# Rows 0 to 5 of a retention and MLP kernel in another form, and the last conversions of w_out placed behind the last burst

## The chip, the cores and the metric

The kernel runs on one core of a Trainium2 chip. The metric is the device time of one execution in microseconds, as a median over runs; a profile of one execution gives the span from its first to its last instruction, engine by engine. The engines are TensorE (PE; its weight loads are listed as PEld), VectorE (DVE), ScalarE (ACT), GpSimd (POOL) and SyncE (SP), which here issues most of the loads.

## The reference

Two computations follow each other. The first is an attention with a decaying state, for 4 batches, 8 heads, 768 tokens and head dimension 64, in float32:

```python
for t in range(S):
    state = gamma * state + einsum("bhd,bhe->bhde", k[:, :, t], v[:, :, t])
    y[:, :, t] = scale * einsum("bhd,bhde->bhe", q[:, :, t], state)
```

`gamma` is 1 - 2**(-5 - head), `scale` is 1/8. The second takes y as x, 3072 tokens of 512 values (8 heads by 64), and computes

```python
h = x @ w_in                      # 512 x 2048
g = h * clip(h + 3, 0, 6) / 6
out = g @ w_out                   # 2048 x 512
```

## The kernel before

**Rows.** The 3072 tokens are 24 rows of 128 tokens, six to a batch. For each row the kernel makes the scores `sc` (keys by queries), multiplies them by a mask that holds decay or causality (`weigh`, result `am`), and sums two parts into `y`: the inner part, from `am` and the values `vn`, and the past part, from the queries and the state. The keys and values of the row are added into the state's PSUM tile `uz` (`sums`), and ACT copies it to a `state` tile in SBUF (`keep`, line 388). A row is worked in two chunks of 64 tokens, so that it needs two state copies, and every product is of 64x64. All these products are issued by `together` (line 384), which deals several lists of products out by turns. In rows 0 to 7 the values are scaled by a decay (`decay`, POOL at line 322 for the rows in ONPOOL, ACT at line 325 for the others) and y by another (`xr`, DVE, line 525); from row 8 on GpSimd scales the keys (line 312) and the queries (line 316, with the table `dq` that SP loads) ahead of the products. Then x is split into a high part (ACT, line 196) and a low part (DVE, line 199), both fp32r.

**h.** Four rows are a unit of 512 tokens; there are six. A weight block of w_in arrives as 64-bit floats in a staging tile `st` (two of them) and is converted by DVE and ACT (lines 160 to 183: `a` and `b` take exponent and mantissa with a mask, `e` is ACT's, then `q`, `f`, `w`) and split into high and low. A tile of h is one block of 128 columns of w_in by one unit: 12 products of 128x128 by 128x512 (line 431: four slices of the inner dimension, and three products of high and low for each). There are 96 tiles. ACT adds 3 and takes the relu (line 438), DVE takes the minimum with 6 and multiplies by h (`times`, line 442), and a DMA that ACT issues stores the tile in DRAM (`gd`, line 465). `finish` is these three steps for one tile.

**o.** The second matrix product (1008 products, line 698) goes over three blocks of 1024 tokens. Each is formed with seven products of half matrices in place of eight, in four groups: (4, 5), (1, 6), (7), (2, 3). A group takes four pieces c0 to c3 of g. A piece is loaded by two SP DMAs into a `gv` tile (lines 668, 671, 673), added or subtracted in DVE (lines 119, 116), and split into a `gc` tile (ACT line 196, DVE line 199). The gv tiles take three places in turn: one in the pool `late`, and `gv0` and `gv1`, which lie in the memory that the staging pool `wst` leaves when phase one ends. The weights of w_out are converted like those of w_in in 16 blocks, with four differences of quarter blocks more (`build_w2`, letters `1230`, and `g k h l` for the splits). Ten of them are made in the long stretch of h, the last six (10 to 15) in unit 5, at tiles 4, 6, 8, 10, 12 and 14 (WHEN).

**What sets the order.** The string HEAD is a fixed list for the first two units: each word is a step (a letter for the step, the row or block or unit.block behind it), and PE, DVE, ACT and SP take their instructions in that order. `steady` does the same for units 2 to 4, with a `chunk_burst` for a row after every fourth tile. In unit 5 and in the o part only PE keeps the written order; a scheduler places the instructions of the others, by priority and by what they depend on, and fixes each engine's list when the kernel is built. Each engine, SP's queue of loads included, takes its list strictly in order. `read` limits the loads in flight to 10 KB in each partition. The stores of h tiles stand in ACT's list behind the next relu (`issue_after`).

Of the kernel before, what the change touches and what calls it, by code (L numbers as in the profile page):

```python
# [30 lines left out]
def retention_ffn(ctx: ExitStack, tc: tile.TileContext, qkv, w_in, w_out, dkc, dqc, dmc, tab, out, B, H, S, D):  # L31
# [784 lines left out]
```

## Time and profile before

| | |
|---|---|
| median of 3 runs | 579.28 us (579.1 to 579.87) |
| profiled execution: own time, span | 581.04 us, 579.3 us |
| PE busy | 565.8 us (98%) |
| DVE busy | 423.8 us (73%) |
| ACT busy | 247.1 us (43%) |
| POOL busy | 45.4 us (8%) |
| on the chain that ended last | h products 44%, o products 40%, the rows' products y, sc, uz 9% together |
| mean DMA rate | 200 GB/s |

A row of the timeline gives start, duration, engine, line, operation, what it writes and reads with shapes, and in square brackets the idle time before it with what ended it. Rows of groups give a count (x1008), the busy time, the mean of one in ns, and the idle time ahead of them. Buffer numbers are left out of the names. A plain float32 product stands in the trace as two passes. The granted clock (PEclk) is TensorE's clock as a share of its full speed.

### The profile page before, as it was taken

To read this page: it belongs to the slowest core of one execution; us is meant where nothing else is said; L and a number is where in the kernel's file an instruction comes from. 1 tells how busy PE (TensorE), PEld (TensorE's weight loads), DVE (VectorE), ACT (ScalarE), POOL (GpSimd) and SP (SyncE) were. 2 spreads that over 40 slices of the span, in tenths; PEclk is the share of its full clock that TensorE was granted. 3 is DMA by queue.
4 is the path that set the end of the run, shared out by engine and by line. 5 is a ranking of instruction groups with operands and counts; after the bars stand their busy time and mean duration, and the time that the engine had idled before them with its cause. 6 is when DMAs were issued, how large, how long until landed. Compare 5 with 4: busy or idle time off the path is not lost.

```text
span 579.3 us, 12415 instructions
## 1 busy us (share of the span) xinstructions
PE 565.8 (98%) x5126; PEld 463.5 (80%) x5126; DVE 423.8 (73%) x588; ACT 247.1 (43%) x368; POOL 45.4 (8%) x51
## 2 busy tenths in 40 slices
PE   7799999999999999999999999999999999999997
PEld 5677887888888888888788888888888888888885
DVE  5489998733677678777726989679776698866871
ACT  3285544432444444434324555543434343344430
POOL 3201011121111111112000000000000000000000
PEclk9799999999999999999999999999999999999999
DMA  8866777835665666666542576465754757636611
GB/s 267 289 212 218 251 250 241 272 132 182 208 212 204 209 218 222 232 221 233 204 158 92 180 246 226 149 216 164 272 180 115 247 148 258 214 107 189 213 74 72
DMA packets 58324, 115.82 MB, mean 200 GB/s; under 512 B 5782, under 2 KB 6678, under 8 KB 58268
## 3 DMA queue, kind: packets, MB, share of 16 engines
q1 hardware_dynamic: 44144, 89.67, 48.1%
q10 hardware_dynamic: 14124, 25.37, 11.6%
q8 instruction: 40, 0.66, 0.5%
q14 instruction: 16, 0.13, 0.1%
HBM read 83.56 MB, written 31.46 MB: 199 GB/s over the span
## 4 chain that ended last, share of the span: by engine, by line
PE 92%; DMA 5%; issue 1%; DVE 1%; SPq 0%; POOL 0%; DVEq 0%
PE h L431 44%; PE o L698 40%; PE y L384 3%; PE sc L384 3%; PE uz L384 3%; DMA early<-in_qkv 2%; DMA st<-in_w_in 2%; DMA qt<-in_qkv 1%; SPq L136 0%; DVE we L160 0%; DVE wb L172 0%; DVE x L199 0%; POOL early L322 0%; DVE xr L525 0%; DVE we L177 0%
## 5 line engine op out<-in xcount | busy, mean ns | idle before, releaser
L431 PE MATMUL h<-x,w 128*128 128x512 f32 x1152 | 270.1, 393 | 0.4 <-ACT w L196 0.3
L431 PEld LDWEIGHTS h<-x,w 128*128 128x128 f32 x1152 | 214.0, 188 | 46.9 <-ACT w L196 0.7
L698 PE MATMUL o<-gc,w 128*128 128x512 f32 x1008 | 230.7, 391 | 0.0
L698 PEld LDWEIGHTS o<-gc,w 128*128 128x128 f32 x1008 | 189.2, 188 | 41.3
L438 ACT ACTIVATE g<-h,three 128x512 f32<-128x512 f32 x96 | 65.8, 687 | 104.2 <-PE h L431 97.6
L442 DVE SCALAR_TENSOR_TENSOR g<-g,h 128x512 f32<-128x512 f32 x96 | 65.5, 684 | 54.8 <-ACT g L438 54.7
L196 ACT ACTIVATE gc<-gv 128x1024 fp32r<-128x1024 f32 x48 | 50.9, 1060 | 63.1 <-PE o L698 56.4
L199 DVE TENSOR_TENSOR gc<-gv,gc 128x1024 fp32r<-128x1024 f32 x48 | 58.6, 1221 | 23.5 <-ACT gc L196 23.5
L196 ACT ACTIVATE gc<-spare 128x1024 fp32r<-128x1024 f32 x36 | 38.2, 1062 | 49.6 <-PE o L698 40.2
L199 DVE TENSOR_TENSOR gc<-spare,gc 128x1024 fp32r<-128x1024 f32 x36 | 43.9, 1221 | 10.3 <-ACT gc L196 10.3
L169 ACT ACTIVATE we<-we,ebias 128x512 int32<-128x512 int32 x32 | 23.0, 719 | 22.2 <-DVE we L160 22.2
L388 ACT ACTIVATE state<-uz 128x256 f32<-128x256 f32 x45 | 17.2, 382 | 29.8 <-PE y L384 16.0
L196 ACT ACTIVATE w<-ww 128x384 fp32r<-128x384 f32 (+2 forms) x34 | 18.6, 552 | 24.3 <-DVE ww L183 23.7
L183 DVE SCALAR_TENSOR_TENSOR ww<-wb,we 128x512 f32<-128x512 f32 x32 | 24.3, 760 | 0.9
L172 DVE SCALAR_TENSOR_TENSOR wb<-st,wb 128x512 f32<-128x512 uint32 x32 | 22.9, 717 | 0.8
L177 DVE SCALAR_TENSOR_TENSOR we<-st,we 128x512 int32<-128x512 int32 x32 | 23.1, 721 | 0.0
L316 POOL TENSOR_TENSOR qs<-qt,dq 128x512 f32<-128x512 f32 x16 | 22.3, 1394 | 3.3 <-DMA dq<-in_decays_q 3.3
L199 DVE TENSOR_TENSOR w<-ww,w 128x384 fp32r<-128x384 f32 (+2 forms) x34 | 20.0, 593 | 2.6 <-ACT w L196 2.5
L160 DVE TENSOR_SCALAR we<-st 128x512 int32<-128x512 int32 x32 | 13.5, 421 | 8.4 <-DMA st<-in_w_in 5.5
L116 DVE TENSOR_TENSOR spare<-spare,gv 128x1024 f32<-128x1024 f32 x12 | 14.7, 1222 | 5.7 <-DMA gv<-gd 5.7
L384 PE MATMUL y<-qs,state 64*64 64x64 f32 x480 | 18.3, 222 | 0.0
L384 PE MATMUL y<-am,vn 64*64 64x64 f32 x512 | 18.2, 219 | 0.0
(66 smaller groups left out, 427.6 us busy)
## 6 DMA issues: line engine op xcount, KB each, us to landing
gd<-g ACTq DMA_DIRECT2D x96, 256.0 KB, 3.0
gv<-gd SPq DMA_DIRECT2D x48, 512.0 KB, 4.8
gv<-gd SPq DMA_DIRECT2D x48, 256.0 KB, 3.1
st<-in_w_in SPq DMA_DIRECT2D x16, 512.0 KB, 4.4
st<-in_w_out SPq DMA_DIRECT2D x16, 512.0 KB, 4.8
early<-in_qkv SPq DMA_DIRECT2D x28, 256.0 KB, 4.3
kt<-in_qkv SPq DMA_DIRECT2D x16, 256.0 KB, 3.4
qt<-in_qkv SPq DMA_DIRECT2D x16, 256.0 KB, 4.1
```

The costliest lines, as they stand in the source:

```text
L169: nc.scalar.activation(out=t["e"], in_=t["e"], func=AF.Relu, scale=8.0, bias=ebias)
L172: nc.vector.scalar_tensor_tensor(out=t["b"].bitcast(F32), in0=lo.bitcast(U32), scalar=2.0**-32, in1=t["b"], op0=ALU.mult, op1=ALU.add)
L177: nc.vector.scalar_tensor_tensor(out=t["e"], in0=hi, scalar=-2147483648, in1=t["e"], op0=ALU.bitwise_and, op1=ALU.bitwise_or)
L183: nc.vector.scalar_tensor_tensor(out=t["w"], in0=t["b"].bitcast(F32), scalar=2.0**-20, in1=t["e"].bitcast(F32), op0=ALU.mult, op1=ALU.mult)
L196: nc.scalar.activation(out=hi, in_=src, func=AF.Copy)
L199: nc.vector.tensor_tensor(out=lo, in0=src, in1=hi, op=ALU.subtract)
L316: nc.gpsimd.tensor_tensor(out=t["qs"], in0=t["qt"], in1=d, op=ALU.mult)
L384: nc.tensor.matmul(out_, lhs, rhs, start=start, stop=True, skip_group_check=True)
L431: nc.tensor.matmul(h, t[:, o, a], xs[u][b][:, k], start=k + n == 0, stop=(k, n) == (NK - 1, 2), skip_group_check=True)
L438: return g, nc.scalar.activation(out=g, in_=h, func=AF.Relu, bias=three).ins
L442: ins = nc.vector.scalar_tensor_tensor(out=g, in0=g, scalar=6.0, in1=h, op0=ALU.min, op1=ALU.mult)
L698: nc.tensor.matmul(acc[i][h] if last else acc[i][:, h], w2c[j][:, RIGHT[i], x, h], gc[:, y, jj], start=j == 0 and n == 0, stop=j == NFP - ...
```

## The change

It has two parts. In the first, rows 0 to 5 are worked whole, 128 tokens at a time. The scores of a row are eight products of 64x128 and eight of 64x64, in an `sc` of two PSUM banks; the mask is 128 wide, and `weigh` multiplies 128x1024 at once. The inner part and the past part are eight products each, the sums eight, with one state copy for each row. The sums of the last row of a batch (row 5) are left out, and its kn isn't read. The values of these rows are laid out by token and scaled with a table `vcst` of their own. Rows 6 and 7, which were in the form of rows 0 to 5, take that of the later rows: GpSimd scales their keys and queries. ONPOOL goes from rows 0 to 4 to rows 1 to 3. One buffer of h tiles in PSUM goes to the scores (ps_h 4 to 3). HEAD is a new list, with other letters for the new steps: O scores, Y past, U inner, N sums, D load of dq, G and R the scaling of keys and queries.

In the second part `build_w2` is given the instruction behind which its first operation has to stand: the last `finish` ahead of it.

```diff
-    ONPOOL = (0, 1, 2, 3, 4)
+    OLD = TROWS
+    ONPOOL = (1, 2, 3)
     HEAD = """
-        L0 L1 F L2 L3 L4 F L5 L6 T0 T1 C0 T3 c0 T4 C1 C3 s0 d0 C4 T5 T2 p0 C5 A0 m0 C2 c1 z1 S1 d1 y0 m1 B0 x0 p1 a0
...
+        L0 L1 F L2 L3 F L4 T1 T0 C1 T2 T4 c0 C2 T3 T5 O0 C4 d0 C5 m0 C0 U0 c1 B0 C3 N0 d1 U1 x0 O1 B1 a0 X0 b0 Y2 q0
...
-    mask = const.tile([P, NPAIR, D], F32, name="mask")
+    mask = const.tile([P, 2, NPAIR // 2, P], F32, name="mask")
...
-    ps_h = ph1.enter_context(tc.tile_pool(name="ps_h", bufs=4, space=PSUM))
+    ps_h = ph1.enter_context(tc.tile_pool(name="ps_h", bufs=3, space=PSUM))
...
-    def build_w2(n):
+    def build_w2(n, after):
         steps = w2_steps(n, fetch(w_out[divmod(n, 2)]))
-        for k in "abeqfw1230gkhl":
+        with tc.issue_after(after):
+            steps["a"]()
+        for k in "beqfw1230gkhl":
             steps[k]()
...
-    sc = ps_a.tile([P, NPAIR, P], F32, name="sc")
+    sc = ps_a.tile([P, 2, NPAIR, P], F32, name="sc")
+    nc.vector.memset(sc, 0.0)
...
+            m = NPAIR * P
+            if x == "kn" and r % ROWS_B == ROWS_B - 1:
+                m = m // 2 if r >= OLD else 0
+            if not m:
+                continue
...
+    def load_q(r):
+
+        d = rows[r]["dqc"] = apool.tile([P, NPAIR, P], F32, tag="dq", name=nm("dq"), bufs=1)
+        read(d.rearrange("p h n -> p (h n)"), dqc[r % ROWS_B])
...
+    def whole_scores(r):
+
+        t, todo = rows[r], []
+        for p in range(NPAIR):
+            for c in range(2):
+                for h, pr in enumerate(halves):
+                    tokens = slice(0, P) if c == 0 else halves[1]
+                    to = sc[halves[h ^ p % 2 ^ c], h, place_am(p, h), tokens]
+                    todo.append((to, t["kt"][pr, p, halves[c]], t["qt"][pr, p, tokens], True))
+        together(todo)
+
+    def whole_past(r):
+
+        y, state, q = both["y"][:, r % 2], before[2 * r], rows[r]["qt"]
+        together([(y[halves[1 - h], p], state[pr, p], q[pr, p], p == 0) for p, h, pr in sides])
+
+    def whole_inner(r):
+
+        t, y = rows[r], both["y"][:, r % 2]
+        first = r % ROWS_B == 0
+        together([(y[halves[1 - h], p], t["vn"][:, p, pr], both["am"][:, h, place_am(p, h)], first and p == 0) for p, h, pr in sides])
+
+    def whole_sums(r):
+
+        t, first = rows[r], r % ROWS_B == 0
+        together([(uz[pr, p], t["kn"][:, p, pr], t["vn"][:, p, pr], first and p == 0) for p, h, pr in sides])
+
+    def whole_weigh(r):
+
+        nc.vector.tensor_tensor(
+            out=both["am"].rearrange("p h a n -> p h (a n)"),
+            in0=sc.rearrange("p h a n -> p h (a n)"),
+            in1=mask.rearrange("p a b n -> p (a b n)")[:, None, :].to_broadcast([P, 2, NPAIR * P]),
+            op=ALU.mult,
+        )
...
             for tile_ in pending[:-1]:
-                finish(*tile_)
+                last = finish(*tile_)
...
-        steady()
+        end = steady()
...
         if jj in WHEN:
-            build_w2(n_w2)
+            build_w2(n_w2, end)
             n_w2 += 1
         end = finish(*tile_of_h(u, jj))
```

The lists of three engines show where this moves instructions. The first is DVE's around the border between the last h tiles and the o part. L442 (now L498) is `times`; `we`, `wb`, `ww`, `ws` are the tiles of a conversion, here of block 15; `w2` is the converted block; `spare` and `gc` belong to pieces of g, whose c0 has gv_517 before and gv_511 now. Before:

```order
L116 TENSOR_TENSOR ws_510_4215<-ww_509_4213,ws_510_4215 128x128
L442 SCALAR_TENSOR_TENSOR g_503_4183<-g_503_4183,h_502_4170 128x512
L116 TENSOR_TENSOR ws_510_4215<-ws_510_4215,ww_509_4213 128x128
L199 TENSOR_TENSOR w2_497_4151<-ww_509_4213,w2_497_4151 128x3x128
L199 TENSOR_TENSOR w2_497_4151<-ws_510_4215,w2_497_4151 128x4x128
L119 TENSOR_TENSOR spare0_4293<-gv_517_4300 128x1024
L442 SCALAR_TENSOR_TENSOR g_505_4200<-g_505_4200,h_504_4187 128x512
L199 TENSOR_TENSOR gc_519_4307<-spare0_4293,gc_519_4307 128x1024
L442 SCALAR_TENSOR_TENSOR g_512_4237<-g_512_4237,h_511_4224 128x512
L442 SCALAR_TENSOR_TENSOR g_514_4254<-g_514_4254,h_513_4241 128x512
L119 TENSOR_TENSOR spare0_4293<-gv_520_4334 128x1024
L199 TENSOR_TENSOR gc_521_4338<-gv_520_4334,gc_521_4338 128x1024
```

Now, where g_506 and g_508 are the last two tiles of h, gv_520 is piece c3, gv_514 is c1, and the first row is block 15's first operation:

```order
L164 TENSOR_SCALAR we_501_4051<-st_500_4049 128x512
L168 TENSOR_SCALAR wb_502_4053<-st_500_4049 128x512
L498 SCALAR_TENSOR_TENSOR g_506_4082<-g_506_4082,h_505_4069 128x512
L176 SCALAR_TENSOR_TENSOR wb_502_4053<-st_500_4049,wb_502_4053 128x512
L181 SCALAR_TENSOR_TENSOR we_501_4051<-st_500_4049,we_501_4051 128x512
L498 SCALAR_TENSOR_TENSOR g_508_4099<-g_508_4099,h_507_4086 128x512
L187 SCALAR_TENSOR_TENSOR ww_503_4058<-wb_502_4053,we_501_4051 128x512
L123 TENSOR_TENSOR spare1_4139<-gv_520_4247 128x1024
L120 TENSOR_TENSOR ws_504_4060<-ww_503_4058 128x128 x2
L120 TENSOR_TENSOR ws_504_4060<-ww_503_4058,ws_504_4060 128x128
L203 TENSOR_TENSOR w2_491_3996<-ww_503_4058,w2_491_3996 128x3x128
L120 TENSOR_TENSOR ws_504_4060<-ws_504_4060,ww_503_4058 128x128
```

Block 15's operations, which stood ahead of the last three `times` with its splits done, now stand among and behind the last two, and behind them come the sum and the split of c3.

The second place is SP's list of loads at the same border. The st tiles are w_out's blocks, L668 (now L716) loads pieces of the first group, L673 (now L721) pieces of the second group. Before, where gv_520, gv_523 and gv_526 are c1, c2 and c3:

```order
L136 DMA st_496_4149<-in_w_out 128x512
L136 DMA st_506_4204<-in_w_out 128x512
L668 DMA gv_520_4334<-gd2_65 128x2x512
L668 DMA gv_520_4334<-gd3_66 128x2x512
L668 DMA gv_523_4368<-gd4_67 128x2x512
L668 DMA gv_523_4368<-gd5_68 128x2x512
L668 DMA gv_526_4402<-gd6_69 128x2x512
L668 DMA gv_526_4402<-gd7_70 128x2x512
L673 DMA gv_531_4440<-gd0_63 128x512
L673 DMA gv_531_4440<-gd1_64 128x512
```

Now, where gv_520 is c3, gv_514 is c1, gv_517 is c2, and gv_531 is c2 of the second group, in the place in `late` that c3 has held:

```order
L140 DMA st_490_3994<-in_w_out 128x512
L140 DMA st_500_4049<-in_w_out 128x512
L716 DMA gv_520_4247<-gd6_69 128x2x512
L716 DMA gv_520_4247<-gd7_70 128x2x512
L721 DMA gv_531_4353<-gd4_67 128x512
L716 DMA gv_514_4179<-gd2_65 128x2x512
L716 DMA gv_514_4179<-gd3_66 128x2x512
L716 DMA gv_517_4213<-gd4_67 128x2x512
L716 DMA gv_517_4213<-gd5_68 128x2x512
L721 DMA gv_531_4353<-gd5_68 128x512
L721 DMA gv_525_4285<-gd0_63 128x512
```

The loads of c1 and c2 moved behind those of c3 and behind the first load of the second group's c2.

The third place is GpSimd's list in the first part of the program. `early` are tiles of rows 0 to 7, am_1 serves as a kn tile. Before:

```order
L322 TENSOR_TENSOR early_3_120<-early_3_120,ccst_71 128x256 x4
L322 TENSOR_TENSOR early_6_132<-early_6_132,ccst_71 128x256 x4
L322 TENSOR_TENSOR early_8_142<-early_8_142,ccst_71 128x256 x2
L312 TENSOR_TENSOR kn_68_878<-kn_68_878,ccst_71 128x512
L316 TENSOR_TENSOR qs_70_883<-qt_66_874,dq_69_881 128x512
L312 TENSOR_TENSOR am_1_118<-am_1_118,ccst_71 128x512
L316 TENSOR_TENSOR qs_99_1043<-qt_96_1035,dq_98_1041 128x512
```

Now:

```order
L348 TENSOR_TENSOR early_3_125<-early_3_125,vcst_71 128x256 x2
L348 TENSOR_TENSOR early_6_137<-early_6_137,vcst_71 128x256 x4
L328 TENSOR_TENSOR early_23_278<-early_23_278,ccst_73 128x512
L334 TENSOR_TENSOR qs_44_550<-early_23_278,dq_24_284 128x512
L328 TENSOR_TENSOR kn_36_459<-kn_36_459,ccst_73 128x512
L334 TENSOR_TENSOR qs_58_656<-early_23_278,dq_45_552 128x512
L328 TENSOR_TENSOR kn_50_562<-kn_50_562,ccst_73 128x512
L334 TENSOR_TENSOR qs_69_764<-qt_48_558,dq_59_658 128x512
```

Four of the ten decays of v have left, and two pairs of scalings of keys and queries, those of rows 6 and 7, stand ahead of the first pair of before.

More of the change, by code (lines that the diff above doesn't have):

```diff
@@ L30, in retention_ffn @@
 @with_exitstack
-def retention_ffn(ctx: ExitStack, tc: tile.TileContext, qkv, w_in, w_out, dkc, dqc, dmc, tab, out, B, H, S, D):
+def retention_ffn(ctx: ExitStack, tc: tile.TileContext, qkv, w_in, w_out, dvs, dkc, dqc, dmc, tab, out, B, H, S, D):
     nc = tc.nc
@@ L266, in retention_ffn @@
     nc.scalar.dma_start(out=bits, in_=tab)
+    nc.scalar.dma_start(out=ccst.rearrange("p n h -> p (n h)"), in_=dkc)
     bits = bits.bitcast(BF16)
@@ L346, in inners, with weigh @@
         return todo
-    def weigh(r, n, table):
+    def weigh(r):
         t = rows[r]
-        t["am"] = chunks(both["am"][:, n])
+        t["am"] = chunks(both["am"][:, 0])
         nc.vector.tensor_tensor(
             out=t["am"].rearrange("p c a t -> p c (a t)"),
-            in0=chunks(sc).rearrange("p c a t -> p c (a t)"),
-            in1=table[:, None, :].to_broadcast([P, 2, NPAIR * D]),
+            in0=chunks(sc[:, r % 2]).rearrange("p c a t -> p c (a t)"),
+            in1=cmask[:, None, :].to_broadcast([P, 2, NPAIR * D]),
             op=ALU.mult,
         )
-    def sums(r, c, q):
-        t, n, y = rows[r], r % ROWS_B, both["y"][:, r % 2]
-        add = [(uz[pr, p], t["kn"][pr, c, p], t["vn"][pr, c, p], n + c + p == 0) for p, h, pr in sides]
-        state = before.get(2 * r + c) if n + c else None
-        past = [
-            (y[halves[1 - h], p, halves[c]], state[pr, p], t[q][pr, p, halves[c]], c + p == 0) for p, h, pr in sides if state is not None
-        ]
-        together(add if n < ROWS_B - 1 or c == 0 else [], past)
     def x_place(r):
@@ L495, in step @@
                 for _ in range(r):
-                    nc.tensor.matmul(both["spare"][:, 0:BLK], mask[:, 0:2], mask, start=True, stop=True)
-            elif kind == "s":
-                together(*scores(r))
-            elif kind == "S":
-                for pair in zip(scores(r), inners(r - 1)):
-                    together(*pair)
-            elif kind == "i":
-                for todo in inners(r):
-                    together(todo)
-            elif kind in "py":
-                sums(r, "py".index(kind), "qt")
-            elif kind in "AB":
-                keep(2 * r + 1 + "AB".index(kind))
+                    nc.tensor.matmul(both["spare"][:, 0:BLK], mask[:, 0, 0], mask[:, 0], start=True, stop=True)
+            elif kind in "OYNU":
+                (whole_scores, whole_past, whole_inner, whole_sums)["OYNU".index(kind)](r)
+            elif kind == "B":
+                keep(2 * r + 2)
+            elif kind in "DGR":
+                (load_q, scale_k, scale_q)["DGR".index(kind)](r)
             elif kind == "P":
-                bursts[r] = later(r)
-                together(bursts[r]["add"][0], bursts[r]["past"][0])
+                lists = later(r)
+                together(lists["add"][0], lists["past"][0])
             elif kind == "Q":
-                chunk_rest(bursts.pop(r) if r in bursts else later(r))
+                chunk_rest(later(r))
             elif kind in "JK":
@@ L582, in steady @@
                 if row + 1 < NROW:
-                    load(row + 1)
+                    next_row(row + 1)
         for tile_ in pending:
             finish(*tile_)
+        return last
     engines = mybir.EngineType
@@ L778, in lay_qkv @@
     q, k, v = (a[:, by_turn(H)] for a in (q, k, v))
-    return np.ascontiguousarray(np.stack([by_dim(q), by_dim(k), by_chunk(k), by_chunk(v)], axis=1))
+    first, later = (np.stack([by_dim(q), by_dim(k), to(k), to(v)], axis=1) for to in (by_token, by_chunk))
+    return np.ascontiguousarray(np.concatenate([first[:TROWS], later[TROWS:]]))
 def lay_w_in(w, H):
```

113 lines of the change are left out of this document (62 added, 51 removed).

## The prediction

> **What bounds the kernel now.** I read the chain of waits first, because it says on which engine the end hangs.
>
> ```profile
> 280.98 1.15 issue
> 295.98 49.19 PE h L431 x216
> 345.17 230.53 PE o L698 x1008
> ```
>
> From 50 us on TensorE is almost never without work: its last 216 h products run straight into the 1008 o products. I call the border E = 345.17 us. Behind E nothing can be won without fewer o products, but a gap at E is paid in full. Two more places are short of work, seen in the busy time by stretch (columns: length; busy time of PE, PEld, DVE, ACT, POOL; granted clock; DMA share; GB/s).
>
> ```profile
> 10.00:50.00 40.00, 32.94 (x950) 27.51 (x943) 28.57 (x48) 21.16 (x56) 5.05 (x7) 0.91 0.78 255
> 15.00:20.00 5.00, 3.94 (x106) 3.61 (x105) 1.61 (x3) 1.29 (x3) 1.64 (x3) 0.66 0.95 302
> 25.00:30.00 5.00, 3.74 (x108) 3.55 (x110) 1.95 (x4) 0.91 (x2) 0.00 (x0) 0.66 0.86 272
> 50.00:80.00 30.00, 30.00 (x221) 24.34 (x222) 29.52 (x49) 14.83 (x25) 4.54 (x4) 1.00 0.71 237
> ```
>
> Between 10 and 50 us PE is idle for 40 - 32.94 = 7.1 us. Twice the granted clock there is 0.66, behind stretches without work: 3.94 x 0.34 and 3.74 x 0.34, together 2.6 us lost. So the head has at most 7.1 + 2.6 = 9.7 us to give. PE's waits up to 50 us say what the idle time is:
>
> ```profile
> PE y L384 <- issue: 1.9, 2, 1.2
> PE sc L384 <- issue: 1.8, 1, 1.8
> PE uz L384 <- issue: 1.6, 3, 0.6
> ```
>
> Of it 1.9 + 1.8 + 1.6 = 5.3 us are waits for nothing that the profile shows. The third place is the 1.15 us at 280.98 above.
>
> **The border between h and o.** This term decides. In DVE's and ACT's timelines (start, duration) the last conversion of w_out, block 15, runs well ahead of E, and so do the loads of gv:
>
> ```profile
> 333.18 0.42 DVE L160 TENSOR_SCALAR we<-st 128x512 int32<-128x512 int32 x1
> 335.66 0.68 DVE L177 SCALAR_TENSOR_TENSOR we<-st,we 128x512 int32<-128x512 int32 x1
> 336.37 7.86 SPq L668 DMA_DIRECT2D gv<-gd  x6
> 341.10 0.68 DVE L442 SCALAR_TENSOR_TENSOR g<-g,h 128x512 f32<-128x512 f32 x1
> 342.32 1.23 DVE L199 TENSOR_TENSOR gc<-spare,gc 128x1024 fp32r<-128x1024 f32 x1 [0.54 <-ACT gc L196]
> 345.79 1.05 ACT L196 ACTIVATE gc<-gv 128x1024 fp32r<-128x1024 f32 x1
> 345.93 0.69 DVE L442 SCALAR_TENSOR_TENSOR g<-g,h 128x512 f32<-128x512 f32 x1 [1.79 <-ACT g L438]
> 347.67 1.22 DVE L199 TENSOR_TENSOR gc<-gv,gc 128x1024 fp32r<-128x1024 f32 x1
> ```
>
> L177 is the last reader of the staging tile, whose memory the gv tiles take; SP starts six gv loads when it runs (336.37). The second piece c1 is ready when its low part ends, at 347.67 + 1.22 = E + 3.7. PE needs it after the 24 products of the first piece; at 230.53 / 1008 = 0.229 us each that is E + 5.5. So 1.8 us are to spare.
>
> Now block 15's first operation stands behind the times of tile (5, 13), which is the row at 341.10 (E - 4.1): 7.9 us later than 333.18, more than four times the spare. Not all of the block moves by as much, so I follow the engines' new order with the durations of these rows and of the groups between 330 and 352 us:
>
> ```profile
> L199 DVE TENSOR_TENSOR w<-ws,w 128x512 fp32r<-128x512 f32 x2 | 1.4, 688 | 0.2 <-ACT w L196 0.2
> L183 DVE SCALAR_TENSOR_TENSOR ww<-wb,we 128x512 f32<-128x512 f32 x2 | 1.4, 690 | 0.0
> L199 DVE TENSOR_TENSOR w<-ww,w 128x384 fp32r<-128x384 f32 x2 | 1.1, 554 | 0.0
> L116 DVE TENSOR_TENSOR ws<-ww 128x128 f32<-128x128 f32 x4 | 1.0, 287 | 0.1
> L119 DVE TENSOR_TENSOR spare<-gv 128x1024 f32<-128x1024 f32 x3 | 3.7, 1219 | 0.0
> gv<-gd SPq DMA_DIRECT2D x6, 512.0 KB, 6.0
> ```
>
> From start to start, successive DVE operations of 128x512 stand 0.60 apart, those of 0.42 us 0.33, those of 128x1024 1.14. Behind the times at E - 4.1 come the low part of c0's sum, which waits for ACT as at 342.32 (E - 2.85 to E - 1.7), a low part of block 14 (to E - 1.1), the block's two mask operations (to E - 0.4), a times, the next two operations of the block (to E + 1.4), the last times, L183's product (to E + 2.7), the sum of c3 (to E + 3.8), differences and a low part (to E + 5.2), and then c3's low part, which ends at E + 6.4.
>
> SP's queue makes this last end count. The first of the loads into gv_531, which belongs to the second group of products, now stands ahead of c1's loads (gv_514), and its tile is the one that c3 leaves with that low part. SP takes its list in order, so c1's loads cannot be issued before E + 6.4. With three issues at about 0.4 us each the second half of c1 leaves at E + 7.3, lands 6.0 us later (E + 13.3), and needs 1.06 us on ACT and 1.22 us on DVE: **c1 is ready at E + 15.6**. PE is dry from E + 5.5: a gap of 10.1 us. If the landing took 4.8 us, the median over the whole page, the gap is 8.9; if crowded loads and a wait at each hand-over add 2 us, it is 12. I take 10.1.
>
> A gap of this size costs clock too: the row 15:20 shows 3.94 busy us at 0.66, so 1.3 us on the restart. Bounds: nothing, and 1.7 us if all of the 5 us stretch had been work (5 x 0.34). That c0 itself is ready at E - 1.7 adds nothing. The border costs 10.1 + 1.3 = **+11.4 us**.
>
> **The gap at 281 us.** The state copy on ACT stood behind a store's issue, which waited for a times on a DVE full of unit 5's conversions:
>
> ```profile
> 280.51 0.68 DVE L442 SCALAR_TENSOR_TENSOR g<-g,h 128x512 f32<-128x512 f32 x1
> 281.22 0.33 ACTq L465 DMA_DIRECT2D gd<-g  x1
> 281.64 0.38 ACT L388 ACTIVATE state<-uz 128x256 f32<-128x256 f32 x1 [1.02 <-DVE w L199]
> ```
>
> These conversions now start behind the last tile ahead of unit 5, so the state copy should follow its sums at once: **-1.2 us** (bounds: -1.2 and 0).
>
> **The head.** Rows 0 to 5 take fewer PE instructions. Each f32 product appears in the trace twice; by the groups of the first 60 us, for 8 rows, a row had 32 score passes, 32 inner, 28 past and 30 sums, 122, and now has 80: 16 scores of 64x128 and 16 of 64x64, 16 inner, 16 past, 16 sums.
>
> ```profile
> L384 PE MATMUL sc<-early 64*64 64x64 f32 x256 | 10.7, 238 | 2.6 <-issue 1.8 <-DMA early<-in_qkv 0.4 <-DVE am L352 0.4
> L384 PE MATMUL y<-early,state 64*64 64x64 f32 x224 | 10.5, 241 | 0.4 <-DVE xr L525 0.4
> L384 PE MATMUL y<-am,early 64*64 64x64 f32 x256 | 10.3, 230 | 1.9 <-issue 1.9
> L384 PE MATMUL uz<-early,kn 64*64 64x64 f32 x112 | 6.3, 251 | 1.1 <-POOL early L322 0.6 <-issue 0.5
> L384 PE MATMUL uz<-early 64*64 64x64 f32 x128 | 5.9, 234 | 1.0 <-issue 1.0
> L352 DVE TENSOR_TENSOR am<-sc,mask 128x512 f32<-128x512 f32 x8 | 5.5, 688 | 5.1 <-PE sc L384 5.0
> L525 DVE TENSOR_TENSOR xr<-y,early 128x512 f32<-128x512 f32 x8 | 5.5, 687 | 4.5 <-PE y L384 4.3 <-PE uz L384 0.2
> 293.97 2.01 PE y L384 x64
> ```
>
> The last row, from the chain, prices a 64x64 pass in a dense burst: 2.01 / 64 = 31 ns, four of them side by side. A pass of 64x128 isn't in the trace: from below 31 ns, if length costs nothing; from above 124 ns, if it streams twice as long and only two fit side by side. For a product over 64 rows I take 62, for the inner product over 128 rows 124, and for sums over 128 rows 62. A row is then 16 x (62 + 31 + 124 + 62 + 62) = 5.5 us against 122 x 31 = 3.8, so 1.7 us more (bounds -1.3, and +2.6 with all the long ones at 124). Rows 0 to 2 hide this under their loads (DMA share 0.95 in 15:20); rows 3 to 5 pay 5.1 us. Against that: the issue waits, if they go with the number of instructions, shrink by 42 / 122 of 5.3, -1.8; with a denser PE the two stretches of low clock should go, -2.6; row 5's kn, 256 KB at 272 GB/s (row 25:30), isn't read, -0.9 (the two dq loads added for rows 6 and 7 come later, where 50:80 shows a DMA share of 0.71); and a row makes one state copy instead of two, one round trip between PE and ACT less, for which I take the 0.38 us of the copy, 6 x 0.38 = -2.3, bounds 0 and twice that. Together 5.1 - 1.8 - 2.6 - 0.9 - 2.3 = **-2.5**, with bounds -6.5 and +5.
>
> The decays of v stay 24 small ones on ACT, and on GpSimd fall from 10 to 6; both wait for loads, so nothing. DVE gets 6 x (1.22 - 0.69) = 3.2 us for the larger weigh and loses two xr, 1.4 us. Between 10 and 50 us it has 40 - 28.57 = 11.4 us free, so I cost this at nothing; were that cover gone, +1.8. GpSimd's scaling of rows 6 and 7 is dearer to DVE than its own time shows:
>
> ```profile
> 49.01 1.09 POOL L312 TENSOR_TENSOR kn<-kn,ccst 128x512 f32<-128x512 f32 x1 [26.06 <-DMA kn<-in_qkv]
> 50.06 1.74 POOL L316 TENSOR_TENSOR qs<-qt,dq 128x512 f32<-128x512 f32 x1
> 49.11 1.53 DVE L172 SCALAR_TENSOR_TENSOR wb<-st,wb 128x512 f32<-128x512 uint32 x1
> 50.68 1.67 DVE L183 SCALAR_TENSOR_TENSOR ww<-wb,we 128x512 f32<-128x512 f32 x1
> ```
>
> Two DVE operations of 0.69 us take 1.53 and 1.67 while GpSimd multiplies: 1.8 us per row, 3.6 for two. They come before 50 us, where DVE has room, but push conversions of w_in into 50:80, where DVE is busy 29.52 of 30 us. I put **+1** into the sum (bounds 0 and 3.6 + 1.8 = 5.4). The Trainium skill, "SBUF — State Buffer", section "SBUF: two separate sides", calls the port pair that DVE and GpSimd share an exclusive lock on which the loser blocks for a whole instruction. These rows agree that DVE stands still, by 1.8 us in two operations.
>
> The fourth ps_h buffer goes to the scores. A tile takes 12 x 0.229 = 2.75 us on PE, and its times ended 0.76 + 0.69 = 1.45 us behind it at E; three buffers allow 5.5. Cost 0; only where DVE is 4 us later than that would PE wait (bounds 0 and 1).
>
> **Sum**, against the profiled span of 579.3 us: -1.2 - 2.5 + 1.0 + 11.4 = +8.7, so 588.0. The execution itself took 581.04, with 1.7 us around the span; the runs' median of 579.28 equals the span, so I predict the median as **588 us**.
>
> **Rivals.** (a) *DVE locked.* The head is worth less than nothing: the longer passes cost their 5.1 us with no idle time won back, and DVE's 5.4 us all reach PE in 50:80. Time 579.3 - 1.2 + 5 + 5.4 - 1 + 11.4, up to 598; at half of it 594. For it: 29.52 of 30. Against: 11.4 us free before. (b) *Half a gap.* The SP queue's order doesn't hold c1 up, which then waits only for L177 in the staging memory, E + 1.4; with 0.9 of issues, 6.0 and 2.3 it is ready at E + 10.6, a gap of 5.1. Time 588 - 5 = 583. Against: gv_531 does stand ahead. (c) *The other side: no gap.* Block 15 runs early enough that c1 stays within its spare. That asks for its loads to be issued by E + 5.5 - 2.3 - 6.0 = E - 2.8, when by the order the block has not begun. Then 579.3 - 1.2 - 2.5 + 1 = 576.6. It decides against me if block 15 starts before E - 7, so that the wait after (5, 13) did not bind. (d) *Code loading is free.* If the issue waits don't depend on how many instructions PE has, the 1.8 stays and the time is 589.8. The Trainium skill, "Runtime: NRT & Kernel Launch", section "Instruction fetch mechanics", says that an engine's code is fetched ahead in blocks of 256 instructions and that crossing into the next is mostly hidden; by it (d) would hold. The three issue rows, with up to 1.8 us for one wait, don't look hidden to me.
>
> **How the numbers follow.** The forecast has 0.48, (a) 0.17, (b) 0.15, (c) 0.07, (d) 0.10; 0.03 stay for a head that gives nearly all 9.7 and a border at half price, 579. The likeliest case by itself runs from 585.5 to 591 (gap 8.9 to 12, head +-1.5). The range for 8 in 10 leaves out (c) and the far half of (a): 582 to 594. Less than 0.2%, 1.2 us, can't be told from no change: faster 0.08, within 0.03, slower 0.89.
>
> **What will show it.** In the changed trace: PE has an idle stretch some 5.5 us after the last h product, 9 to 12 us long, which ends on DVE's or ACT's gc of c1, itself behind SP's load; the first conversion of block 15 stands behind the times of (5, 13); SP's wait ahead of gv_531 ends on a DVE gc; the granted clock drops behind the gap. The state copy of the row at 281 us has no wait. In 10:50 PE's idle time is under 7 us and its issue rows sum to 3 to 4 us. I am wrong if the end of h moves by more than 5 us, or if PE runs from h into o without a gap.

## The result, and the profile after

The changed kernel takes 595.44 us (median of 4 runs, 594.35 to 596.26), the kernel before 579.19 us on the same chip (578.26 to 579.87): a ratio of 1.0281 (95% interval 1.0255 to 1.0306), 16.25 us slower (14.8 to 17.7). The forecast was slower by 8.7 us, at 588, with a range up to 594. The sign and the place were right; the size was not, and the time lies 1.4 us outside the range.

The profiled execution of the changed kernel has a span of 594.6 us against 579.3. Its chain of waits around the border between h and o (start, length, what):

```profile
295.94 49.19 PE h L487 x216
345.13 5.61 PE o L746 x24
350.81 1.06 ACT gc L200
351.90 1.24 DVE gc L203
353.15 0.34 SPq L721
353.60 0.52 SPq L716
354.16 6.00 DMA gv<-gd
360.26 1.23 DVE spare L123
361.48 1.15 DVE gc L203
362.67 228.25 PE o L746 x983
```

The h products end at 345.13 us, before at 345.17: everything ahead of the border comes out even. All of the 15.3 us lie behind it. After the 24 products of c0 PE waits through the whole circle: c3's split on ACT and DVE, the issue of gv_531 (L721) that stood behind it, then c1's loads (L716), their 6.00 us of transfer, and c1's split. Two rows of ACT's timeline show who held c3's split:

```profile
350.81 1.06 ACT L200 ACTIVATE gc<-gv 128x1024 fp32r<-128x1024 f32 x1 [1.66 <-PE o L746]
360.25 1.06 ACT L200 ACTIVATE gc<-gv 128x1024 fp32r<-128x1024 f32 x1 [7.86 <-DMA gv<-gd]
```

The first is c3's. It waited for PE: the gc tiles take five places in turn, and c3's first one falls on the second of c0, which PE still reads. So c3's split could not begin before PE had finished c0, and c1's load, which PE needed next, stood behind it in SP's list. With this order the stall could not have been shorter than that chain.

By stretch (length; busy time of PE, PEld, DVE, ACT, POOL; granted clock; DMA share; GB/s):

```profile
10.00:50.00 40.00, 33.80 (x691) 27.37 (x689) 35.84 (x53) 17.89 (x44) 10.41 (x10) 0.96 0.85 276
40.00:50.00 10.00, 6.87 (x200) 5.11 (x198) 9.96 (x14) 3.43 (x8) 4.49 (x4) 1.00 0.79 258
50.00:80.00 30.00, 30.00 (x297) 24.63 (x289) 29.45 (x48) 14.99 (x25) 3.57 (x3) 1.00 0.65 219
351.00:361.00 10.00, 0.00 (x0) 0.00 (x0) 2.58 (x4) 2.14 (x3) 0.00 (x0) 0.67 0.66 210
361.00:368.00 7.00, 6.12 (x14) 4.45 (x15) 6.77 (x7) 3.65 (x5) 0.00 (x0) 0.50 0.55 179
```

PE does nothing for 10 us and then takes up work at half clock, until 368 us. In the head PE's idle time went from 7.1 us to 6.2, but DVE went from 28.57 us busy to 35.84 of 40: its free time of 11.4 us, which the prediction counted as cover, is down to 4.2, and GpSimd's time there has doubled. In 50:80 PE is busy throughout, as before.

The 15.3 us can be taken apart from the starts of the o products in the two traces (first to last: 230.29 us before, 245.55 after):

| part of the o products | forecast | after |
|---|---|---|
| gap before the first product of c1, above the usual 0.229 | 10.1 | 10.8 |
| slow start behind it (13 intervals, mostly 0.43 in place of 0.229) | 1.3 | 3.6 |
| 0.8 us spread evenly over all 1008 products | not seen | 0.8 |

### The profile page after: what moved, and what is told of

It reads as the page before. It is cut to its first block, busy times and chain, and to the rows that moved or that the text cites. A ratio compares the mean times of both kernels' runs of the same rounds, so it can differ in the third digit from the quotient of the medians.

```text
span 594.6 us, 11798 instructions
## 1 busy us (share of the span) xinstructions
PE 570.5 (96%) x4832; PEld 464.2 (78%) x4832; DVE 426.8 (72%) x587; ACT 244.0 (41%) x362; POOL 50.3 (8%) x53
## 4 chain that ended last, share of the span: by engine, by line
PE 84%; DMA 9%; DVE 4%; SPq 1%; issue 1%; ACT 0%; POOL 0%; DVEq 0%; POOLq 0%; ACTq 0%
PE o L746 39%; PE h L487 39%; DMA st<-in_w_in 4%; DMA early<-in_qkv 3%; PE uz L440 2%; PE sc L440 2%; PE y L440 2%; DMA gv<-gd 1%; DMA qt<-in_qkv 1%; SPq L140 1%; DVE wb L176 1%; DMA dq<-in_decays_q 1%; DVE g L498 1%; DVE w L203 1%; DMA am<-in_qkv 0%
## 5 line engine op out<-in xcount | busy, mean ns | idle before, releaser
L746 PE MATMUL o<-gc,w 128*128 128x512 f32 x1008 | 234.8, 395 | 11.2 <-ACT gc L200 10.6
L498 DVE SCALAR_TENSOR_TENSOR g<-g,h 128x512 f32<-128x512 f32 x96 | 65.6, 685 | 57.3 <-ACT g L494 57.1
L444 ACT ACTIVATE state<-uz 128x256 f32<-128x256 f32 x39 | 14.9, 383 | 26.8 <-PE y L440 18.1
L181 DVE SCALAR_TENSOR_TENSOR we<-st,we 128x512 int32<-128x512 int32 x32 | 24.1, 753 | 1.4 <-ACT we L173 1.4
L187 DVE SCALAR_TENSOR_TENSOR ww<-wb,we 128x512 f32<-128x512 f32 x32 | 23.0, 719 | 0.8
L440 PE MATMUL y<-qs,state 64*64 64x64 f32 x528 | 20.3, 222 | 1.7 <-DVE x L203 1.7
L123 DVE TENSOR_TENSOR spare<-gv 128x1024 f32<-128x1024 f32 x12 | 14.7, 1222 | 10.2 <-DMA gv<-gd 10.2
```

The lines of the kernel that those rows point to most:

```text
L181: nc.vector.scalar_tensor_tensor(out=t["e"], in0=hi, scalar=-2147483648, in1=t["e"], op0=ALU.bitwise_and, op1=ALU.bitwise_or)
L187: nc.vector.scalar_tensor_tensor(out=t["w"], in0=t["b"].bitcast(F32), scalar=2.0**-20, in1=t["e"].bitcast(F32), op0=ALU.mult, op1=ALU.mult)
L440: nc.tensor.matmul(out_, lhs, rhs, start=start, stop=True, skip_group_check=True)
L498: ins = nc.vector.scalar_tensor_tensor(out=g, in0=g, scalar=6.0, in1=h, op0=ALU.min, op1=ALU.mult)
L746: nc.tensor.matmul(acc[i][h] if last else acc[i][:, h], w2c[j][:, RIGHT[i], x, h], gc[:, y, jj], start=j == 0 and n == 0, stop=j == NFP - ...
```

## The experiments

Time ratios are against the kernel before, on the same chip, with their 95% intervals. On these chips executions of the kernel before lay between 577.4 and 585.4 us, and in the traces of kernels that share its head product 96 of h (counted from 0) starts anywhere from 60.7 to 65.1 us, so the head of a single trace says little. For the border I compare the first-to-last time of the o products in the traces: it was 230.29 us in every trace of a kernel with the old rows and no gap, but for the one with a spacer, below.

### The two parts apart

The changed kernel with the second part undone (rows alone, e1):

```diff
-        with tc.issue_after(after):
-            steps["a"]()
-        for k in "beqfw1230gkhl":
+        for k in "abeqfw1230gkhl":
             steps[k]()
```

> The changed kernel with the second part undone: block 15's first operation has no instruction that it must follow; rows 0 to 7 stay in their new form. Theory: the stall between h and o hangs on that placement alone, and with it go 15.1 us of o; the gap at 281 us, which was 1.0 shorter, comes back. Time 594.4 - 15.1 + 1.0 = 580.3 (579 to 582), PE runs from h into o without idle time. Rival: the new form of the rows changes what the scheduler makes of the rest, and the stall stays in part: over 588.

The kernel before with the second part only (wait alone, e2):

```diff
+        with tc.issue_after(after):
+            steps["a"]()
-        for k in "abeqfw1230gkhl":
+        for k in "beqfw1230gkhl":
             steps[k]()
...
-            build_w2(n_w2)
+            build_w2(n_w2, end)
```

> The kernel before with only the second part of the change: block by block, the first operation of a conversion in unit 5 stands behind the last finish ahead of it. Theory: border +15.1, gap at 281 us -1.0, so 593.3 (592 to 595), with c1's load behind a load of the second group in SP's list. Rival: without the new rows the border stays as it was, under 585.

Rows alone: 583.49 us, ratio 1.0057 (1.0027 to 1.0086), and o without a gap, 231.09 us. Run once more beside other kernels:

> The kernel of e1 once more, beside the others, to tell what the new form of the rows costs by itself against the kernel before: theory +1 us from the trace of the changed kernel, e1 measured +3.3 (1.6 to 4.9).

586.41 us, ratio 1.0126 (1.0072 to 1.0180): the two intervals together say +1.6 to +10 us for the rows alone, where I expected +1 and 580.3 us. Wait alone: 592.44 us, ratio 1.0212 (1.0169 to 1.0255), as expected, with o at 245.37 us. Its chain is that of the changed kernel, though its rows are the old ones:

```profile
346.44 1.07 ACT gc L196
347.53 1.24 DVE gc L199
349.80 6.66 DMA gv<-gd
358.96 227.49 PE o L701 x983
```

So the stall hangs on the placement of the conversions alone, and the rival that the new rows bring it falls.

### The circle in SP's list

The changed kernel, with the loads of the second group held behind c2's last load (loads in turn, e3):

```diff
                         if g == 0:
-                            nc.sync.dma_start(out=gv[:, :, jj], in_=gd[j][:, :, t0 + UT : t0 + TB])
+                            ins = nc.sync.dma_start(out=gv[:, :, jj], in_=gd[j][:, :, t0 + UT : t0 + TB]).ins
+                            if c == 2:
+                                c2_load = ins
...
+                    elif sb == 0 and g == 1:
+                        first.enter_context(tc.issue_after(c2_load))
```

> The changed kernel with one more rule: the loads of the second group of the first block of tokens stand behind c2's last load in SP's list, so that c1's load no longer waits for c3's split. Theory: the circle in SP's list (c1's load behind gv_531, that behind c3's split, that behind PE's products of c0) makes 10.6 us of idle time; without it c1's load goes when block 15's L181 ends, 347.4 us, lands some 6 us behind its two issues (354.4), and is split at 356.7; PE is dry from 350.7, a gap of 6.0, and loses 2 to 3 us of clock: 594.4 - 15.1 + 8.3 = 587.6 (585.5 to 589.5). Rival 1, the list's order is harmless: 594.4. Rival 2, the list's order is all: 579 to 581.

590.0 us, ratio 1.0165 (1.0116 to 1.0214). The time is 0.5 us above the expected stretch; in the profiled execution h ends 1.4 us later than in the changed kernel. The o products took 238.26 us, 7.97 more than the usual 230.29, where 8.3 were expected. In its chain SP issues c1's loads as soon as block 15's L181 has read the staging tile:

```profile
348.19 0.61 DVE we L181
348.81 0.52 SPq L718
349.38 5.83 DMA gv<-gd
356.53 1.15 DVE gc L203
```

So of the 15.3 us 7.3 belong to the circle in SP's list and 7.2 to block 15's lateness itself; the other 0.8 has another source, shown below. Both rivals fall.

The other way round, the changed kernel with the blocks asked for four tiles sooner, the rule kept (e7):

```diff
-    WHEN = (4, 6, 8, 10, 12, 14)
+    WHEN = (0, 2, 4, 6, 8, 10)
```

> The changed kernel with unit 5's blocks of w_out asked for four tiles sooner (at tiles 0, 2, 4, 6, 8, 10 in place of 4 to 14), the rule on the first operation kept. SP's list then has c1, c2, c3 and the second group in turn, and block 15 is done ahead of the last h tiles. Theory: lateness is the cause and the list's order its effect, so PE runs from h into o with no idle time, or under 1.5 us: 594.4 - 15.1 = 579.3 up to 581.5, plus what the chip's start costs. Rival: the rule holds the blocks back whatever the tile, and some 5 us or more of idle time stay: over 586.

PE runs from h into o without a gap:

```profile
293.47 49.19 PE h L487 x216
342.65 231.33 PE o L746 x1008
```

The profiled execution has a span of 577.6 us; the median is 583.91, ratio 1.0058 (1.0023 to 1.0093), the same as for the rows alone. With the blocks sooner the list's order mends itself: the lateness is the cause, the circle its effect. What remains is the price of the rows.

### What the rows cost

Rows 6 and 7 without GpSimd's scaling, on top of the rows alone (e5). This leaves out a part of the computation and serves only to price it:

```diff
-        nc.gpsimd.tensor_tensor(out=k, in0=k, in1=ccst[:, n, 0:a, None].to_broadcast([P, a, D]), op=ALU.mult)
+        if r not in (6, 7):
+            nc.gpsimd.tensor_tensor(out=k, in0=k, in1=ccst[:, n, 0:a, None].to_broadcast([P, a, D]), op=ALU.mult)
...
+        if r in (6, 7):
+            t["qs"] = t["qt"]
+            t.pop("dqc")
+            return
```

> The kernel of e1 (rows in the new form, w_out's conversions not held) without GpSimd's scaling of the keys and queries of rows 6 and 7; the products of these rows take them unscaled, so this leaves out part of the computation. All loads stay. Theory: between 39 and 52 us four multiplications on GpSimd make four DVE operations 0.84 to 1.08 us longer, 3.9 us together, at a time when DVE has no idle time and PE waits for it: product 48 of h starts 3 to 4 us earlier than in e1, DVE's long operations between 39 and 52 us are gone, and the time falls by 3 to 4 us against e1. Rival 1, the loss sits in the longer passes of PE or in the loads: product 48 and the time as in e1 (within 1 us). Rival 2, the cover further on takes it back: product 48 earlier by 3, time by under 1.

580.27 us, ratio 1.0013 (0.9986 to 1.0040): against 583.49 and 586.41 for the rows alone that is 3 to 6 us less, and no longer told from the kernel before. Its interval lies below that of the second run of the rows alone and overlaps a little with that of the first. The traces say the same more directly. From the first h product to product 96, between which the same row products lie in all of these kernels, the one without the scaling takes 32.3 us; the five traces with the same head list and the scaling (the changed kernel, e1 twice, e3 and e7) take 34.4 to 37.1. So the scaling costs 2.1 to 4.8 us there, as the theory has it.

Where it costs them is only partly what was expected. First, in the changed kernel, GpSimd's four multiplications for rows 6 and 7 and the DVE operations that meet them:

```profile
33.25 1.47 POOL L328 TENSOR_TENSOR early<-early,ccst 128x512 f32<-128x512 f32 x1 [13.71 <-DMA dq<-in_decays_q]
34.26 1.01 DVE L181 SCALAR_TENSOR_TENSOR we<-st,we 128x512 int32<-128x512 int32 x1 [0.44 <-ACT we L173]
34.69 1.73 POOL L334 TENSOR_TENSOR qs<-early,dq 128x512 f32<-128x512 f32 x1
39.91 1.05 POOL L328 TENSOR_TENSOR kn<-kn,ccst 128x512 f32<-128x512 f32 x1 [3.50 <-DMA kn<-in_qkv]
39.93 1.58 DVE L176 SCALAR_TENSOR_TENSOR wb<-st,wb 128x512 f32<-128x512 uint32 x1
40.92 1.73 POOL L334 TENSOR_TENSOR qs<-early,dq 128x512 f32<-128x512 f32 x1
41.43 1.77 DVE L203 TENSOR_TENSOR x<-xr,x 128x512 fp32r<-128x512 f32 x1
```

Three DVE operations of some 0.69 us take 1.01, 1.58 and 1.77: 2.3 us more, and 2.7 and 3.1 in the traces of e7 and e1. The next pair on GpSimd, at 46.34 and 49.45, is row 8's. The kernel before has it too (49.01 and 50.06), and the kernel without the scaling keeps it (46.05 and 47.05), with DVE operations of 1.28 and 1.77 us beside it. So two of the four long operations that the expectation adds up to 3.9 us were never at stake. In PE's waits up to 50 us of the changed kernel's execution DVE stands where "issue" stood before. The last two of these rows are single waits that end at 49.2 and 44.5 us, behind the long operations:

```profile
PE y L440 <- DVE am L392: 1.8, 3, 0.9
PE y L440 <- DVE x L203: 1.7, 1, 1.7
PE h L487 <- DVE w L203: 1.4, 1, 1.4
```

Then the stretches 40:50 and 50:60, of the rows alone and without the scaling:

```profile
40.00:50.00 10.00, 6.90 (x149) 4.84 (x147) 9.90 (x15) 4.30 (x9) 4.84 (x4) 1.00 0.69 231
50.00:60.00 10.00, 9.50 (x120) 8.05 (x121) 8.83 (x16) 4.63 (x8) 0.00 (x0) 0.83 0.39 129
```

```profile
40.00:50.00 10.00, 9.21 (x246) 7.43 (x246) 9.90 (x17) 5.12 (x11) 2.73 (x2) 1.00 0.64 214
50.00:60.00 10.00, 10.00 (x46) 8.24 (x45) 9.83 (x19) 4.46 (x8) 0.00 (x0) 1.00 0.61 207
```

DVE is busy 9.90 us of 10 in 40:50 in both, but PE 6.90 against 9.21. In this execution of the rows alone TensorE's clock also fell to half for 3.4 us (0.83 in the next stretch); in the profile of the changed kernel it did not. The eight traces with the new rows fall into two sets. In e1 twice, e3 and e8 the clock falls to half for 3.4 us somewhere between 47 and 56 us, and product 96 of h starts at 67.0 to 68.9 us. In the changed kernel, e5, e7 and e10 it does not, and product 96 starts at 62.5 to 65.1. That may be why kernels with the new rows spread more (580 to 585 us for the rows alone, where 15 of 18 runs of the kernel before on that chip lay between 578 and 582); it is argued, not shown, and how much of the scaling's price goes through the clock stays open.

Could the scaling be had more cheaply? On ACT and DVE, on top of the rows alone (e8):

```diff
+        if r in (6, 7):
+            for i in range(a):
+                nc.scalar.activation(out=k[:, i], in_=k[:, i], func=AF.Copy, scale=ccst[:, n, i : i + 1])
+            return
...
-        nc.gpsimd.tensor_tensor(out=t["qs"], in0=t["qt"], in1=t.pop("dqc"), op=ALU.mult)
+        eng = nc.vector if r in (6, 7) else nc.gpsimd
+        eng.tensor_tensor(out=t["qs"], in0=t["qt"], in1=t.pop("dqc"), op=ALU.mult)
```

> The kernel of e1 with the scaling of rows 6 and 7 moved: the keys by ACT (eight operations of 128x64 per row, 0.34 us each), the queries by DVE (one of 0.69 us per row). Nothing is left out. Theory: DVE loses 3.9 us of waiting for GpSimd and gets 1.4 us of work, ACT gets 5.4 us between 33 and 50 us, where it is busy about half: 1 to 2.5 us less than e1. Rival: in their fixed lists the new operations wait for their loads and hold up what stands behind them, so 0 or slower than e1.

583.04 us, ratio 1.0081 (1.0049 to 1.0113): no gain that can be told from the rows alone. ACT's new work of 2.02 us stands in its list ahead of a step that a conversion on DVE needs:

```profile
33.35 2.02 ACT L328 ACTIVATE early<-early,ccst 128x64 f32<-128x64 f32 x8
36.53 0.69 DVE L181 SCALAR_TENSOR_TENSOR we<-st,we 128x512 int32<-128x512 int32 x1 [2.57 <-ACT we L173]
```

On DVE alone, on top of the blocks asked for sooner (both `nc.gpsimd` of the scaling become `nc.vector` for rows 6 and 7; e10):

> The kernel of e7 (the change with blocks asked for sooner) with the keys and the queries of rows 6 and 7 scaled by DVE itself, 0.69 us each, in place of GpSimd. Nothing is left out. Theory: 2.8 us of work take the place of some 4 us in which DVE stands, so 1 to 2 us less than e7 (median 583.9, ratio 1.0058): ratio 1.002 to 1.004. Rival: the operations wait in DVE's fixed list for their loads, as ACT's did in e8: no gain or slower than e7.

580.3 us, ratio 1.0022 (0.9998 to 1.0046), against 583.91 and 1.0058 with GpSimd: as expected, but the two intervals overlap, and in the traces the stretch from the first h product to product 96 is no shorter (35.3 us, with GpSimd in e7 34.4). That DVE's own 0.69 us is the cheaper way isn't shown.

One more part of the first change by itself, three buffers for h tiles in the kernel before (`ps_h`, `bufs=4` to `bufs=3`; e6):

> The kernel before with ps_h 3 in place of 4, nothing else. As the prediction has it: 0, bounds 0 and 1, so 579.2 to 580.2. Rival: in the first 100 us, where DVE has no time free, the times of a tile stand more than a tile behind PE, and PE waits for a buffer: 581 to 583.

581.43 us, ratio 1.0010 (0.9980 to 1.0040): no cost that can be told, as forecast. This was with the old rows; with the new ones it wasn't tried.

### The 0.8 us in all o products

Every trace with the new rows and no gap (e1 twice, e5, e7, e8, e10) has 231.09 us from the first to the last o product, every one with the old rows so far (before, e6) 230.29. Two variants of the kernel before tell what of the change does it. With a spacer among the constants, ahead of nearly everything in SBUF (e11):

```diff
+    spacer = const.tile([P, 304], F32, name="spacer")
+    nc.gpsimd.memset(spacer, 0.0)
```

> The kernel before with an unused constant tile of 304 floats in each partition, what the change's wider mask and vcst add, so that all later tiles in SBUF lie 1216 bytes further on. The 1008 o products take 231.1 us from first to last start in every kernel with the new rows that has no gap (e1, e5, e7, e8, e10) and 230.3 in every one with the old rows (before, e6, e9). If the place of the tiles in SBUF makes the difference: 231.1. If it is something else in the program: 230.3.

And with PSUM laid out as in the changed kernel (e12):

```diff
-    ps_h = ph1.enter_context(tc.tile_pool(name="ps_h", bufs=4, space=PSUM))
+    ps_h = ph1.enter_context(tc.tile_pool(name="ps_h", bufs=3, space=PSUM))
...
-    sc = ps_a.tile([P, NPAIR, P], F32, name="sc")
+    sc2 = ps_a.tile([P, 2, NPAIR, P], F32, name="sc")
+    nc.vector.memset(sc2, 0.0)
+    sc = sc2[:, 0]
```

> The kernel before with the scores' tile in two PSUM banks (the second stays zero and unused) and ps_h 3, so that PSUM is laid out as in the changed kernel. If the place of the o accumulators in PSUM makes the 0.8 us in the o products: 231.1 from first to last start; else 230.3.

The chains' o rows, of the spacer and of the two banks:

```profile
342.01 231.33 PE o L700 x1008
```

```profile
343.04 230.53 PE o L700 x1008
```

The spacer alone reproduces the 0.8 us to the hundredth, the PSUM layout does nothing. (Single times of 578.67 and 578.94 us beside 580.73 for the kernel before; the head's spread covers such a difference.)

### Blocks sooner, with the old rows

The kernel before with the second part, and the blocks asked for at tiles 0 to 10 (e9):

> The kernel before with the rule on the first operation of unit 5's conversions, and these blocks asked for four tiles sooner (tiles 0 to 10); rows 0 to 7 stay in their old form. Theory: with c1, c2 and c3 in turn the border costs nothing, as in e7, and what the rule wins at 281 us stays: 0.9 us less than before, 578.5 (577.5 to 579.5). Rival 1: the shorter stretch at 281 us was the spread from one execution to the next, 279.4, no change. Rival 2: block 15 is still too late for c1 and PE idles: 581 or more.

579.29 us, ratio 1.0012 (0.9986 to 1.0038); o without a gap, 230.29 us. It is no faster than before, so the gain of 0.9 us at 281 us isn't shown; the interval reaches down to 0.8 us less. No version that was run beats the kernel before.

## Why the prediction was right or wrong

**The border: right in mechanism and sign, too small.** The forecast followed the engines' lists to +11.4 us; the trace has +15.3. Its steps, one by one:

- *c3's low part ends at E + 6.4*: it ended at 353.13, E + 8.0. The forecast let it wait for DVE's list only. It missed that a gc tile of c3 takes the place of one that PE reads until E + 5.6 (the ACT row with 1.66 <-PE). From there the two splits, 1.06 and 1.23, follow one another.
- *SP issues c1 behind gv_531, 6.0 us of landing*: 6.00 in the chain, from 354.16, E + 9.0 (forecast E + 7.3).
- *c1 ready at E + 15.6*: PE took its first product of c1 at 361.35, E + 16.2, since that product needs only the high part, and went on at 362.67, E + 17.5. The gap was 10.8 for 10.1.
- *The restart, 1.3 us, at most 1.7*: 3.6. This is the step of the border that failed most. The price came from a stretch of 5 us with a mean clock of 0.66, in which the clock was at half for only 3.4 us (15.7 to 19.1 us of the kernel before). Behind the gap it stayed at half until 368 us:

```profile
350.70:354.30 3.60, 0.03 (x1) 0.00 (x0) 2.13 (x4) 1.58 (x2) 0.00 (x0) 1.00 0.07 5
354.40:367.90 13.50, 6.02 (x13) 4.42 (x14) 7.42 (x7) 4.30 (x5) 0.00 (x0) 0.50 0.74 243
368.10:372.00 3.90, 3.90 (x19) 3.23 (x18) 3.13 (x4) 1.86 (x2) 0.00 (x0) 1.00 0.22 78
```

 From the first product of c1 to the next it takes 1.32 us, then 0.59, and the next 11 intervals, up to 367.96, are 0.43, nearly twice the usual. The wait alone, with a gap of 11.4, lost the same 3.6; the kernel with loads in turn, with a gap of 4.5, lost 2.7.
- *Nothing for the place of the tiles*: 0.8, by the spacer.

**The head: forecast -2.5 and +1.0; in the trace of the change no gain, and over many runs worse.** From product 63 of h on, the same row products are still to do before and after the change, so that the two kernels can be compared. Product 96 starts at 65.13 us, before at 65.11 (in the six traces with the old rows at 60.7 to 65.1). By product 840 the change is 1.0 us behind (269.21 against 268.25), but that stretch takes 202.2 to 204.5 us over all fourteen traces, with old rows and new. By the intervals the rows alone cost +1.6 us at least. Two steps failed.

- *The longer passes, 5.5 us a row*: dense bursts in the changed kernel show a row's four steps, from start to start 0.51 for the sums, 1.05 for the inner part, 0.84 for the scores, about 1.0 for the past.

```profile
26.92 0.69 PE L440 MATMUL uz<-early 128*64 128x64 f32 x16
27.43 1.05 PE L440 MATMUL y<-am,early 128*64 128x128 f32 x16
28.48 0.90 PE L440 MATMUL sc<-early 64*64 64x128 f32 x32
30.21 1.09 PE L440 MATMUL y<-early,state 64*64 64x128 f32 x16
```

 That is 3.4 us, below the 3.8 of the old form and not 1.7 above it. The inner product costs 51 ns a pass where I took 124 (0.82 us over 16). The 5.1 us for them were nothing, and the idle time that was to pay for them did not come back either: the "issue" waits are gone, but with DVE's waits in their place PE's idle time in 10:50 is 6.2 us against 7.1.
- *DVE's 11.4 us free are cover*: much of that was free time of an engine that waited for PE. In the first 60 us DVE's waits ahead of `am` and `xr` were 5.1 and 4.5 us before, nearly all for PE; now they are 0.6 and 2.0. DVE became the bound from 40 us on (9.96 of 10 in 40:50, 8.23 before), and there GpSimd's scaling cost 2.1 to 4.8 us, where +1 stood in the sum. Without the scaling the rows cost 0.8 us (-0.8 to 2.3). Rival (a), at 0.17, had this part of the mechanism right, with a place that was 10 us too late; its 5.1 us for the longer passes was as wrong as mine. (Its terms add up to 598.9, not 598, and the 256 KB of row 5's kn at 272 GB/s are 0.96 us, not 0.9.)

**The gap at 281 us: -1.2 forecast, -1.0 in the trace, for the wrong reason.** The state copy was to follow its sums at once. It stands at the same time as before, 281.63 against 281.64:

```profile
281.63 0.38 ACT L444 ACTIVATE state<-uz 128x256 f32<-128x256 f32 x1 [0.29 <-DVE w L203]
```

What changed is that its sums came 1.0 us later, as all of PE's work did by then. Over all traces the stretch from product 864 to 888 takes 7.6 to 8.7 us with the rule (six) and 7.9 to 10.0 without (eight); a gain of 0.8 in the mean, with as much spread. Its cause stays open.

**Of the other rivals**, (b), half a gap, is what the kernel with loads in turn does (gap 4.5, forecast 5.1, and the clock on top); the list's order did hold c1 up, so the changed kernel doesn't. (c) falls. For (d): PE's "issue" waits up to 50 us were 5.3 us before with 122 passes a row; in the changed kernel, with 80, none stands in the list of waits. With the old rows they differ from one execution to the next: 3.1 us in the wait alone. The Trainium skill, "Runtime: NRT & Kernel Launch", section "Instruction fetch mechanics", calls the crossing from one block of code into the next mostly hidden. Here the waits went away with the instructions, which speaks against it for this head, but no run here isolates them, and the time they gave back went into waits for DVE.

**The range.** The trace's +15.2 us are 6.5 more than the forecast's 8.7: 3.0 from the gap and its restart, 0.8 from the place of the tiles, 2.5 from the head, 0.2 from the gap at 281 us. The range's lower end took in half a gap; its upper end of 594 left out that a slower restart, the tile that PE held and a head that wins nothing could come together.

## What to carry to other kernels

When a list of instructions is made anew, follow the whole circle at the first place where PE must not wait: not only which engine is late, but which tile's place each load and each split needs, and who still reads there; one load of a later group ahead of the next piece turns a lateness of a few us into a serial chain of transfer, split and restart. An engine's free time is cover only as long as it comes from waiting for a slower one: give that one less to do, and the cover is gone where it was counted. And asking for the late work sooner (four tiles here) repaired the border, where a rule on its order alone had broken it.

## What the runs showed of the hardware that was not expected

- After 10.8 to 11.4 us without work TensorE ran its next products at half pace, 0.43 us in place of 0.229, until 5.3 us after they began to follow one another; after 4.5 us without work, until 3.3 us after. The Trainium skill, "TensorE: Matmul & The Clock Gate", section "What's actually happening", has the clock fall after an idle window of about 3.4 us and rise after as long a busy one; here the clock was still whole in 350.7:354.3, the first 3.6 us without work, and 0.50 from 354.4 to 367.9, so these lengths agree with it, with up to 2 us more on the rise.
- Moving the tiles in SBUF by 1216 bytes in each partition, with nothing else changed, made 1008 products 0.8 us longer (0.35%); the traces with the new rows, which add as much, show the same to the hundredth. Which tile's place matters stays open.
- A float32 pass of 128 columns over 128 rows cost 51 ns in a dense burst, against 31 for the dense 64x64 passes that the prediction used.
